# A fused pooling-attention and ResMLP kernel: the channel MLP cut into 512-token blocks across batch borders, q and k loaded as fp32 rows and cast on chip, the next batch's attention spread over both MLP products

## The chip, the cores and the metric

One core of a Trainium2 chip runs the whole kernel in one launch. The metric is device time in microseconds (us), the median of several executions. In the profile PE is TensorE's matmuls, PEld its weight loads, DVE VectorE, ACT ScalarE, POOL GpSimd, SP SyncE. A *period* below is the time from the first matmul of one MLP block's first product to that of the next block; I read these starts from the traces.

## The reference, cut to what matters

```python
# q, k, v: 8 batches x 8 heads x 576 tokens x 64, fp32
k_p = k.reshape(B, H, 72, 8, D).mean(axis=3)        # pooling by 8
v_p = v.reshape(B, H, 72, 8, D).mean(axis=3)
attn = softmax(scale * q @ k_p.T)
x = (attn @ v_p)  ->  (B, 576, 512)
tok = einsum('ts,bsd->btd', w_tok, alpha1 * x + beta1)   # token mix, 576 x 576
u = x + lam * tok
out = u + lam * (relu((alpha2 * u + beta2) @ w_ch1) @ w_ch2)   # channel MLP, 512 -> 2048 -> 512
```

## The kernel before

One batch of 576 tokens is one MLP block. TensorE's instruction stream weaves the MLP of batch b-1 with the attention of batch b; all engines take their instructions in a fixed order that a scheduler decides at build time. The parts that the argument touches (cuts marked):

```python
CR = [128, 128, 128, 128, 64]                  # token chunks of one batch

def load_qk_dma(b):                            # casting transfers: rows of 64 values
    for src, dst in ((q, q_bf), (k, k_bf)):
        for c in range(NCH):
            nc.gpsimd.dma_start(out=dst[0:rows, hf, c, :]..., in_=src[b, :, 128*c:128*c+rows, :]...)
...
nc.vector.memset(q_bf[64:65, :, 4, :], 0.0)    # a 65th row of zeros under the 64 remaining tokens
nc.vector.memset(k_bf[64:65, :, 4, :], 0.0)
...
def blk_F(b, hp):                              # the "q/k block", four per batch
    ...                                        # four transposes of q, 128 rows each
    nc.tensor.transpose(out=ps_qb[0:P, 0:65], in_=q_bf[0:65, hf, 4, h0:h0 + 128],
                        identity=identity_bf[0:65, 0:65])
    ...                                        # four pooling matmuls of k, 128 rows each
    nc.tensor.matmul(out=ps_kp[0:P, 64:72], lhsT=k_bf[0:65, hf, 4, h0:h0 + 128],
                     rhs=poolmat[0:65, 0:8])
...
def blk_V(b, hp):                              # the "v sums", two per head pair, on VectorE
    for hh in range(2):
        nc.vector.tensor_reduce(out=vp1[:, hh, 0:64], in_=v_hp[:, hh]..., op=ALU.add)
...
def blk_A(b, j):                               # first product: two halves of 288 columns
    for cc in range(4):
        for half in range(2):
            nc.tensor.matmul(out=ps_h[half][0:P, 0:288], lhsT=w1raw[:, cc, P*j:P*j+P],
                             rhs=u_fm[:, cc, n0:n0 + 288], ...)
    for half in range(2):
        nc.scalar.activation(out=Hj[:, n0:n0 + 288], in_=ps_h[half][0:P, 0:288], func=AF.Relu, ...)
...
def blk_B(b, tcx):                             # second product: five chunks, the last of 64 tokens
    for j in range(NJ):
        nc.tensor.matmul(out=ps_ch[0:tr, 0:DM], lhsT=s["Hj"][j][:, CO[tcx]:CO[tcx] + tr],
                         rhs=w2l[:, j, :], ...)
```

The softmax here doesn't subtract the row's maximum and nothing guards it: scores larger than these inputs give would overflow.

## Time and profile before

| | before |
|---|---|
| time, median | 438.4 us (438.4 to 439.0) |
| span of the profiled run, granted TensorE clock | 437.3 us, 0.973 |
| first MLP matmul | 62.0 us |
| period, batches 1 to 5 | 48.2 us |
| TensorE / VectorE / ScalarE busy | 89% / 52% / 46% |

TensorE is the bound, after a prologue in which it has little to do. The prediction shows the lines for that. Two more lines of the profile matter later. The first is the count of DMA packets:

```profile
DMA packets 88371, 35.37 MB, mean 81 GB/s; under 512 B 77776, under 2 KB 79824, under 8 KB 88336
```

The second is one q/k block in the timeline of TensorE in the kernel before. The columns are the start, the time until the group's last end, engine, line, operation, out<-in, the rows and columns of the array that the weights take, and the shape.

```profile
207.78 0.40 PE L209 MATMUL ps_qa<-identity_bf,q_bf 128*128 128x128 bf16 x4
208.02 0.20 PE L213 MATMUL ps_qb<-identity_bf,q_bf 65*128 65x65 bf16 x1
208.05 0.25 PE L220 MATMUL ps_kp<-poolmat,k_bf 128*128 128x16 bf16 x4
208.16 0.17 PE L222 MATMUL ps_kp<-poolmat,k_bf 65*128 65x8 bf16 x1
```

Matmuls overlap, so their durations must not be added; the starts tell what each costs. The 65-row transpose holds TensorE from 208.02 to 208.05 us, about 30 ns, and the whole block until the next MLP matmul, at 208.18 us, takes 0.40 us.

### The profile page before, as it was taken

How to read it: one execution, taken by the hardware profiler on the slowest of the kernel's cores; microseconds unless marked ns; L12 is line 12 of the kernel's file. 1: busy time of each engine (PE TensorE's matmuls, PEld its weight loads, DVE VectorE, ACT ScalarE, POOL GpSimd, SP SyncE). 2: the span in 40 equal slices, each digit the busy share in tenths (PEclk: the TensorE clock that was granted, in tenths of full speed). 3: DMA queues.
4: the chain of work that ended last, by engine and by line, in shares of the span. 5: the costliest groups of instructions: out<-in, count | busy, mean ns of one | idle time of the engine just before them, and what ended most of it. 6: DMA issues, size and time to landing. Idle time of an engine off the chain costs nothing.

```text
span 437.3 us, 7370 instructions
## 1 busy us (share of the span) xinstructions
PE 387.7 (89%) x2881; PEld 237.6 (54%) x2881; DVE 229.3 (52%) x598; ACT 202.6 (46%) x564; POOL 96.0 (22%) x128
## 2 busy tenths in 40 slices
PE   0166769999899989998999989998999989998996
PEld 0045257644675457644774457544764467545742
DVE  2378795776167643666077633874177514444011
ACT  1055139701892059602991079403980189205910
POOL 7574442810044000810063002700000000000000
PEclk9995779999999999999999999999999999999999
DMA  9999999972059200941089200921001100010011
GB/s 130 220 174 207 214 177 162 111 151 64 2 53 176 86 12 1 140 145 43 2 76 164 75 13 19 166 80 36 1 1 72 38 1 1 36 63 12 1 48 61
DMA packets 88371, 35.37 MB, mean 81 GB/s; under 512 B 77776, under 2 KB 79824, under 8 KB 88336
## 3 DMA queue, kind: packets, MB, share of 16 engines
q0 software_dynamic: 81280, 23.08, 48.7%
q1 hardware_dynamic: 5248, 9.44, 6.3%
q10 hardware_dynamic: 1808, 2.38, 2.0%
q8 instruction: 22, 0.36, 0.3%
q14 instruction: 13, 0.11, 0.1%
HBM read 39.08 MB, written 9.44 MB: 111 GB/s over the span
## 4 chain that ended last, share of the span: by engine, by line
PE 69%; DVE 12%; ACT 11%; DMA 4%; POOL 2%; issue 2%; POOLq 0%
PE ps_ch L346 29%; PE ps_h L331 23%; PE ps_tok L302 8%; ACT Hj L337 6%; DVE u_bf L308 3%; DVE out_sb L306 3%; PE ps_sc L247 3%; DMA k_bf<-in_k_dram 2%; DVE vp L233 2%; ACT ET L250 2%; PE ps_uT L317 2%; PE ps_av L263 2%; ACT qT L211 1%; DMA wt_sb<-in_moe_w_tok_dram 1%; DVE out_sb L350 1%
## 5 line engine op out<-in xcount | busy, mean ns | idle before, releaser
L331 PE MATMUL ps_h<-u_fm,w1raw 128*128 128x288 bf16 x1024 | 149.9, 288 | 1.1
L346 PE MATMUL ps_ch<-w2l,Hj 128*128 128x512 bf16 (+1 forms) x640 | 146.4, 379 | 0.0
L337 ACT ACTIVATE Hj<-ps_h,bias_cols 128x288 bf16<-128x288 f32 x256 | 113.0, 502 | 7.7 <-PE ps_h L331 5.2
L331 PEld LDWEIGHTS <-w1raw 128*128 128x128 bf16 x1024 | 96.8, 98 | 33.8 <-issue 6.0
L346 PEld LDWEIGHTS <-Hj 128*128 128x128 bf16 (+1 forms) x640 | 61.6, 100 | 66.1 <-issue 0.4
L320 ACT COPY u_fm<-ps_uT 128x512 bf16<-128x512 bf16 (+1 forms) x40 | 21.7, 542 | 157.8 <-PE ps_uT L317 157.8
L233 DVE TENSOR_REDUCE vp<-v_hp 72x64 f16<-72x512 f32 x64 | 63.9, 1007 | 7.0 <-DMA v_hp<-in_v_dram 7.0
L350 DVE TENSOR_TENSOR out_sb<-out_sb,ps_ch 128x512 f32<-128x512 f32 (+1 forms) x40 | 27.4, 685 | 73.2 <-PE ps_ch L346 73.1
L270 DVE RECIPROCAL rec<-ps_av 128x4 f32<-128x4 f32 x64 | 11.3, 177 | 92.6 <-PE ps_av L266 92.6
L79 POOL DMA_DIRECT2D v_hp<-in_v_dram x32 | 22.6, 708 | 164.8 <-DVE vp L233 159.3
L302 PE MATMUL ps_tok<-xs_tm,wtT 128*128 128x512 bf16 (+3 forms) x200 | 51.9, 393 | 4.6 <-DVE xs_tm L279 3.9
L250 ACT ACTIVATE ET<-ps_sc 72x288 f16<-72x288 f32 x128 | 44.7, 408 | 19.9 <-PE ps_sc L247 19.7
L306 DVE TENSOR_TENSOR out_sb<-x_tm,ps_tok 128x512 f32<-128x512 f32 (+1 forms) x40 | 27.3, 683 | 18.3 <-PE ps_tok L302 18.0
L63 POOL DMA_DIRECT2D k_bf<-in_k_dram x40 | 33.8, 890 | 8.8 <-DMA w2raw<-in_moe_w_ch_dram 3.5
L63 POOL DMA_DIRECT2D q_bf<-in_q_dram x40 | 34.1, 873 | 6.2 <-DMA v_hp<-in_v_dram 3.4
L302 PEld LDWEIGHTS <-wtT 128*128 128x128 bf16 (+3 forms) x200 | 18.4, 102 | 28.6 <-issue 9.1
L209 PE MATMUL ps_qa<-identity_bf,q_bf 128*128 128x128 bf16 x128 | 14.1, 236 | 16.4 <-POOL identity_bf L105 12.9
L317 PE MATMUL ps_uT<-identity_bf,u_bf 128*128 128x128 bf16 (+1 forms) x160 | 15.0, 216 | 15.1 <-DVE u_bf L308 15.1
L308 DVE TENSOR_TENSOR u_bf<-out_sb,al_bc 128x512 bf16<-128x512 f32 (+1 forms) x40 | 27.5, 688 | 1.2
L247 PE MATMUL ps_sc<-qT,kpT 128*72 128x288 bf16 x128 | 28.1, 305 | 0.0
L273 DVE TENSOR_TENSOR x_tm<-ps_av,rec 128x256 f32<-128x256 f32 x64 | 26.1, 408 | 0.0
L279 DVE TENSOR_TENSOR xs_tm<-x_tm,lamal_bc 128x256 bf16<-128x256 f32 x64 | 26.1, 407 | 0.0
(54 smaller groups left out, 244.5 us busy)
## 6 DMA issues: line engine op xcount, KB each, us to landing
v_hp<-in_v_dram POOLq DMA_DIRECT2D x32, 288.0 KB, 4.8
out_dram<-out_sb SPq DMA_DIRECT2D x32, 256.0 KB, 2.0
q_bf<-in_q_dram POOLq DMA_DIRECT2D x32, 128.0 KB, 4.4
k_bf<-in_k_dram POOLq DMA_DIRECT2D x32, 128.0 KB, 4.5
w1raw<-in_moe_w_ch_dram POOLq DMA_DIRECT2D x4, 512.0 KB, 11.0
w2raw<-in_moe_w_ch_dram POOLq DMA_DIRECT2D x4, 512.0 KB, 15.0
wt_sb<-in_moe_w_tok_dram ACTq DMA_DIRECT2D x4, 288.0 KB, 9.6
out_dram<-out_sb SPq DMA_DIRECT2D x8, 128.0 KB, 2.2
```

Source lines behind the costliest of these rows:

```text
L63: nc.gpsimd.dma_start(out=dst[0:rows, hf, c, :].rearrange("p (h d) -> p h d", d=D), in_=src[b, :, 128 * c:128 * c + rows, :].rearrange("h ...
L233: nc.vector.tensor_reduce(out=vp1[:, hh, 0:64], in_=v_hp[:, hh].rearrange("g p d -> g d p"), axis=mybir.AxisListType.X, op=ALU.add)
L247: nc.tensor.matmul(out=ps_sc[0:SPg, 0:288], lhsT=kpT[:, hh, :], rhs=qT[:, n0:n0 + 288])
L250: nc.scalar.activation(out=ET[:, n0:n0 + 288], in_=ps_sc[0:SPg, 0:288], func=AF.Exp, bias=0.0, scale=0.125)
L273: nc.vector.tensor_tensor(out=x_tm[:, 0:4, dd:dd + 64], in0=av[:, 0:4, 0:64], in1=rec[:, 0:4].unsqueeze(2).to_broadcast((P, 4, 64)), op=AL ...
L302: nc.tensor.matmul(out=ps_tok[0:tr, 0:DM], lhsT=wtT[0:kk, sc, CO[tcx]:CO[tcx] + tr], rhs=xs_tm[0:kk, sc, :], start=(sc == 0), stop=(sc == 4))
L306: nc.vector.tensor_tensor(out=s["out_sb"][0:tr, tcx, :], in0=st["x_tm"][0:tr, tcx, :], in1=ps_tok[0:tr, 0:DM], op=ALU.add)
L308: nc.vector.tensor_tensor(out=s["u_bf"][0:tr, tcx, :], in0=s["out_sb"][0:tr, tcx, :], in1=al2_bc[0:tr, :], op=ALU.mult)
L331: nc.tensor.matmul(out=ps_h[half][0:P, 0:288], lhsT=w1raw[:, cc, P * j:P * j + P], rhs=u_fm[:, cc, n0:n0 + 288], start=(cc == 0), stop=(cc ...
L337: nc.scalar.activation(out=Hj[:, n0:n0 + 288], in_=ps_h[half][0:P, 0:288], func=AF.Relu, bias=bias_cols[:, j:j + 1], scale=1.0)
L346: nc.tensor.matmul(out=ps_ch[0:tr, 0:DM], lhsT=s["Hj"][j][:, CO[tcx]:CO[tcx] + tr], rhs=w2l[:, j, :], start=(j == 0), stop=(j == NJ - 1))
L350: nc.vector.tensor_tensor(out=s["out_sb"][0:tr, tcx, :], in0=s["out_sb"][0:tr, tcx, :], in1=ps_ch[0:tr, 0:DM], op=ALU.add)
```

## The change

The intent: cut 4608 tokens into nine blocks of 512 instead of eight of 576 (the fifth chunk of 64 tokens wasted half of each matmul); evict 512 columns with one ScalarE instruction instead of two of 288; load q and k in wide fp32 rows on a hardware queue and cast on chip; and place the attention of the next batch beside both MLP products instead of mostly the first. The kernel was rewritten; this is the core of the diff, with cuts marked "...".

```diff
-        for src, dst in ((q, q_bf), (k, k_bf)):
-                nc.gpsimd.dma_start(
-                    out=dst[0:rows, hf, c, :].rearrange("p (h d) -> p h d", d=D),
...
+            nc.sync.dma_start(
+                out=raw[:, i, :, 0:4, :].rearrange("p h c d -> p h (c d)"),
+                in_=two[:, 0:512, :].rearrange("h (p c) d -> p h (c d)", c=4))
...
+            eng.tensor_copy(out=bf[:, i, 0:4].rearrange("p c h d -> p h c d"),
+                            in_=raw[:, i, :, 0:4, :])
+            eng.tensor_copy(out=bf[0:REM, i, 4], in_=raw[0:REM, i, :, 4, :])
...
-            nc.tensor.transpose(... in_=q_bf[0:65, hf, 4, h0:h0 + 128], identity=identity_bf[0:65, 0:65])
+        nc.tensor.transpose(out=ps_q[0:P, 512:576], in_=bf[0:REM, 0, 4],
+                            identity=identity_bf[0:REM, 0:REM])
...
+    for b in range(0, B, 2):
+        chunks += [(b, c) for c in range(4)]
+        chunks += [(b + 1, c) for c in range(4)]
+        chunks += [(b, 4)]
...
-                                 rhs=u_fm[:, cc, n0:n0 + 288],
+            nc.tensor.matmul(out=ps_h, lhsT=w1[:, cc, P * j:P * j + P], rhs=u_fm[n][:, cc, :],
+                             start=(cc == 0), stop=(cc == 3))
...
+        for hp in range(4):
+            todo.append((-1.0 + 3.5 * hp, lambda hp=hp: cast_qk(b, hp, (nc.gpsimd, nc.gpsimd))))
+            todo.append((1.5 + 3.5 * hp, lambda hp=hp: att_F(b, hp)))
+            todo.append((2.0 + 3.5 * hp, lambda hp=hp: att_V(b, hp)))
+        for h in range(H):
+            todo.append((14.5 + 1.0 * h, lambda h=h: att_S(b, h)))
+            todo.append((16.6 + 1.0 * h, lambda h=h: att_AV(b, h)))
```

REM is 64. A chunk (b, 4) holds the remainders of two batches. The numbers in the last lines are positions among the 32 steps of one MLP block (16 of the first product, 16 of the second); they set the program's order only, and the scheduler, which builds each engine's queue from it, may still move an instruction where its inputs allow it.

## The prediction

> **What bounds the kernel now.** I read the page's engine and slice rows first, then busy time by stage, then the chain of work that ended last, in order of time.
>
> ```profile
> PE 387.7 (89%) x2881; PEld 237.6 (54%) x2881; DVE 229.3 (52%) x598; ACT 202.6 (46%) x564; POOL 96.0 (22%) x128
> ...
> PE   0166769999899989998999989998999989998996
> PEclk9995779999999999999999999999999999999999
> DMA  9999999972059200941089200921001100010011
> ```
>
> TensorE is busy for nine tenths of nearly every slice from the seventh on, at the full clock; the DMA engines are full for the first 75 us and mostly idle afterwards. So there are three regimes, and the stage table (span, then PE, PEld, DVE, ACT, POOL busy, granted clock, DMA share, GB/s) separates them:
>
> ```profile
> 0.00:62.00 62.00, 27.93 (x240) 18.51 (x241) 39.44 (x99) 16.79 (x49) 34.78 (x51) 0.84 1.43 189
> ...
> 206.80:255.00 48.20, 46.56 (x349) 28.29 (x349) 26.49 (x71) 24.48 (x70) 11.20 (x14) 1.00 0.55 74
> ...
> 399.90:437.30 37.40, 33.23 (x210) 20.35 (x208) 3.43 (x5) 14.73 (x33) 0.00 (x0) 1.00 0.09 32
> ```
>
> A prologue of 62 us, until the first channel-MLP matmul; seven periods of 48.2 us, one batch's MLP woven with the next batch's attention; a tail of 37.4 us with MLP alone. The tail gives clean matmul prices:
>
> ```profile
> 399.93 15.81 PE ps_h L331 x128
> 415.74 17.40 PE ps_ch L346 x80
> ```
>
> 15.81 us / 128 = 123.5 ns for 288 columns and 217.5 ns for 512; inside a stage eight of the first kind take 0.98 us (122.5 ns) and sixteen of the second 3.46 us (216.3 ns). The same chain inside a period shows what PE waits for:
>
> ```profile
> 206.82 0.69 DVE u_bf L308
> 207.57 0.30 PE ps_uT L317 x4
> 207.89 0.37 ACT u_fm L320
> 208.26 0.54 ACT qT L211
> 209.27 0.33 ACT Hj L337
> 209.67 0.49 ACT Hj L337
> 210.16 0.47 ACT qT L211
> 211.09 1.67 ACT Hj L337 x4
> 212.76 0.58 ACT ET L250 x2
> ```
>
> At the batch border it is VectorE (the last chunk of u) and then, for the first 7 us of the first product, ScalarE's evictions, not TensorE. A price list for one period (timeline starts, next to next): first product 128 x 0.1225 = 15.7; second 80 x 0.2163 = 17.3; token mix 25 x 0.216 = 5.4; scores 8 x 0.24 = 1.9; attention times v 8 x 0.15 = 1.2; q transpose and k pooling 4 x 0.40 = 1.6; transposes of u 1.1. Sum 44.2, so **4.0 us of each 48.2 us period is TensorE waiting**, although "busy" shows only 1.6 us of idle, because busy durations overlap.
>
> **What the Trainium skill says.** "TensorE: Matmul & The Clock Gate", section Back-to-back issue gap, gives N/2.4 + 2.5 ns for a warm matmul: 122.5 and 215.8 ns for 288 and 512 columns, and the trace agrees (122.5, 216.3). The same section also says a stream sustains about 131 ns at N = 512; this trace does not, and I use 216.3. The price does not depend on the number of rows of the result, so the 64-token fifth chunk costs a full 128-row one: 16 x 216 ns = 3.46 us per batch (the chain has 3.57 for it). "VectorE: DVE Perf Modes", section The TRN2 errata, gives ScalarE 172 + N cycles at 1.2 GHz from PSUM: 383 ns for 288, 570 ns for 512. Four evictions of 288 take 1.67 us in the chain, about 0.39 apart: agreement. "DMA: Bandwidth & Descriptors", section Specifications, asks for at least 512 B for line rate. The trace agrees in kind: of 88,371 packets 77,776 are under 512 B, nearly all of them q and k rows of 64 bf16 values, and their queue is busy 48.7% of the engines' time. "GPSIMD Engine Reference", section Engine selection, calls one-input elementwise work on GpSimd roughly line rate; no run here shows a cast there yet.
>
> **The change part by part.**
>
> *MLP in nine blocks of 512 tokens.* The 4608 tokens become 9 x 512 instead of 8 x 576, two 64-token remainders sharing a chunk. First product: 9 x 64 x 0.2163 = 124.6 us instead of 8 x 15.7 = 125.4. Second: 9 x 64 x 0.2163 = 124.6 instead of 8 x 17.3 = 138.4. **Saved on TensorE: 14.7 us**, on the path.
>
> *One 512-wide eviction instead of two of 288.* In the old first product ScalarE has 32 x 0.39 = 12.5 us of ReLU, about 4 x 1.0 us of q, k copies and 14 x 0.29 us of exp: 20.6 us, in a phase that lasts 21.1 us. It is as full as TensorE there. New: 16 x 0.57 = 9.1 plus 4 x 0.65 of qT = 11.7 us, against 13.8 + 1.6 us of TensorE. The exps move beside the second product, kpT copies go to VectorE. ScalarE stops binding.
>
> *Spread attention.* VectorE's work in a period is about 28 us, as before (v sums 8 us, x 4.5, xs 3, u and output 10). The instruction order of the built kernel has 19 second-product matmuls (4.1 us) between the last attention times v and the token mix; VectorE's chain for x and xs in that gap is about 3 us (two v sums included), so it should be hidden. After the first two mixes 7 more matmuls (1.5 us) hide the conversion of u. Exposed I expect the last transposes of u, 0.5 to 1 us. TensorE's sum per period: 13.84 + 13.84 + 5.4 + 1.9 + 1.2 + 1.6 + 1.0 = 38.8. I add 1.4 us of waits by judgement, a third of what the old one has: **40.2 us**.
>
> *q, k as fp32 rows, cast on chip.* Packets of 256 B read and 128 B written become 1 KB. By packet durations (32 ns for the old kind; 86 to 98 ns for 1 to 2 KB) a batch's q and k fall from 19 to about 9 us of all engines. In the steady part that was hidden and is worth nothing; casts on GpSimd, some 10 us in 40 (my estimate), are hidden too. It counts in the prologue alone.
>
> *Prologue.* Data first: batch 0 is 3.5 MB, w_tok 1.3, then w1, w2 (8.4 MB at the source) and batch 1's 3.5 MB compete; the old kernel moves about 190 GB/s as landed there. The last piece needed, batch 1's first v, which VectorE's order places before the last u, should land near 45 to 50 us. VectorE: 13 v sums x 0.93 = 12.1, u 8 x 0.65 = 5.2, x 4.2, xs 2.9, w_tok's sums and copies 6.5, casts 2.4, kpT and qT 2.8, one w2 scaling 2.2, constants 2.2: 40.5 us, starting near 9 us where the old one gets its first broadcast rows (9.90). With 4 us of waits, last transpose and copy: **53.5 us** to the first MLP matmul, against 62.2.
>
> *Sum.* 53.5 + 7 x 40.2 = 281.4, plus 2.4 in block 0 (a mix of 1.1, bias columns 1.3), two blocks with MLP alone 2 x 27.7 = 55.4, a tail of 4.2 after the last matmul as before (437.3 - 433.1), and 1.1 from span to time (438.4 - 437.3): **398.0 us**. Of the 40.4 us gained, 14.7 are matmuls saved, about 18 waits (7 x 2.6), 8.7 the prologue, less 2.
>
> **Rivals.**
>
> *VectorE becomes the bound of the second product.* It gets x, xs, u, output and v sums in about 25 us, some 20 us of it busy; a late xs stalls the mix. For it: v sums stand between urgent work in its order, and the old chain already has v sum, x, xs ahead of the mix (240.99 to 242.78). Against: 19 matmuls of cover. It would make the period 42 to 43 and the time 412.
>
> *The prologue stays bound by transfers.* The same bytes from HBM, w1 and w2 early, [...]and DMA engines that were full. Then the first MLP matmul comes at 60 to 62 and the time is 406. Against: q and k packets were the slow ones.
>
> *Nothing stalls.* 38.9 us a period and a prologue of 49: 384 us.
>
> *The transfer change pays in every period.* Against: from 158 us on the DMA engines are half idle and no long wait on q, k or v is listed. I give it nothing.
>
> **Range and chances.** Prologue 53.5 +6/-5, periods 281.4 +13/-8; taken as independent, with the matmul savings certain, 387 to 411 holds 8 in 10. For less than 2% gain the time would have to exceed 429.7, which needs both rivals and more: 0.03. Slower: 0.01.
>
> **What would show it right or wrong.** First-product matmuls at 216 ns, x576, one ReLU of 512 columns below 0.6 us start to start; a period of 40 us with ScalarE gone from the chain in the first product; the first MLP matmul near 53.5 us with VectorE in the chain before it. Wrong if the chain of a period shows xs or v sums ahead of the mix for over 2 us, GpSimd casts ahead of q's transposes, or transfers of v or w_tok in the prologue after 50 us.

## The result, and the profile after

The changed kernel took **439.1 us** (437.6 to 439.9, 4 runs), the kernel before 438.7 us (438.4 to 439.3) on the same chip: a ratio of 1.000, 95% interval 0.998 to 1.003. (Ratios in this document are the mean time of one kernel's fast runs over that of the other's in the same rounds, so not quite the ratio of the medians.) The expected gain of 40 us did not come, though less work was done, as the page of the changed kernel shows (its busy row of TensorE, the row of the granted clock in 40 slices, the packets):

```profile
PE 370.4 (85%) x2315; PEld 191.5 (44%) x2358; DVE 233.2 (53%) x484; ACT 181.8 (42%) x348; POOL 71.9 (17%) x139
...
PEclk9999859999999999999999999999999999999999
...
DMA packets 43436, 44.71 MB, mean 103 GB/s; under 512 B 12624, under 2 KB 33104, under 8 KB 43408
```

TensorE is busy 17 us less, ScalarE 21 us less, and the packets are halved; the time went into waiting. The stage table (as in the prediction: start and end, length, busy time of PE, PEld, DVE, ACT and POOL, granted clock, DMA share, GB/s) says where: prologue, blocks 4 and 6, and the first block with MLP alone.

```profile
0.00:64.46 64.46, 25.68 (x178) 17.05 (x180) 42.84 (x113) 12.87 (x29) 23.68 (x44) 0.89 1.03 228
245.27:290.68 45.41, 41.03 (x265) 21.19 (x269) 26.89 (x54) 20.63 (x40) 6.56 (x16) 1.00 0.25 77
333.78:375.49 41.71, 40.70 (x266) 21.22 (x270) 20.39 (x46) 20.63 (x40) 0.00 (x0) 1.00 0.08 26
375.49:403.11 27.62, 27.52 (x129) 12.51 (x129) 2.48 (x4) 11.58 (x17) 0.00 (x0) 1.00 0.10 39
```

The block with MLP alone takes 27.62 us (27.7 predicted). The prologue is 11 us longer than predicted. And of two blocks with the same work, block 4 takes 3.7 us more than block 6; the differences visible here are VectorE, 26.89 against 20.39 us busy, and GpSimd, 6.56 us against none (its casts for a later batch). Three things can be read from the trace before any experiment.

**The q/k block costs twice what it did.** TensorE's timeline in the changed kernel, to be held against the one of before:

```profile
215.79 0.39 PE L233 MATMUL ps_q<-identity_bf,qk_bf 128*128 128x128 bf16 x4
216.11 0.20 PE L235 MATMUL ps_q<-identity_bf,qk_bf 64*128 64x64 bf16 x1
216.24 0.29 PE L245 MATMUL ps_kp<-pool_main,qk_bf 128*128 128x64 bf16 x4
216.46 0.18 PE L247 MATMUL ps_kp<-pool_rem,qk_bf 64*128 64x8 bf16 x1
216.57 0.61 PE L351 MATMUL ps_h<-u_fm,w 128*128 128x512 bf16 x2
```

From start to start the remainder's transpose now holds TensorE 0.13 us (0.03 before) and the whole block 0.78 us (0.40 before), although it is the same number of matmuls. Two differences are visible: "64*128" where "65*128" stood, since the kernel before carried a 65th row of zeros, and 64 columns instead of 16 in the pooling of k (e1 below keeps the 64 columns and so tests the rows alone). The Trainium skill, "TensorEngine Tiling (Array Packing)", section Key Properties, says that a change of tiling mode drains TensorE; its section Available Configurations lists 64 x 128 under row tiling, apart from 128 x 128. My reading is that 65 rows fall into the 128-row mode and 64 don't; four switches a block at about 0.1 us are the 0.38 us (each of the four starts after a switch comes 0.08 to 0.11 us later than in the kernel before, counted from the start before it).

**VectorE has the v sums in the wrong place.** Waits of TensorE and VectorE in block 4 of the changed kernel (total us, how often, the longest; 245 to 291 us), and then the chain of work at the end of block 3 (start, us, what):

```profile
DVE kpT L249 <- PE ps_kp L247: 12.1, 4, 3.8
...
PE ps_uT L340 <- DVE u_bf L329: 2.2, 2, 1.3
PE ps_tok L324 <- DVE xs L297: 1.8, 1, 1.8
```

```profile
233.41 0.92 DVE vp L256
234.32 0.60 DVE xs L297
...
235.12 0.60 DVE u_sb L369
235.72 1.87 DVE vp L256 x2
237.60 1.19 DVE u_sb L327 x2
238.79 0.61 DVE u_bf L329
239.45 0.40 PE ps_uT L340 x4
```

VectorE stands idle 12.1 us in the first product, waiting for the next pooled k, while TensorE waits 4.0 us for xs and u in the second, where sums ("vp") of the *next* batch stand ahead of them in VectorE's queue. VectorE doesn't wait for v there, so v had landed; the scheduler put the sums where it found room (my reading of its order). All eight sums of a period lie in the second product in blocks 0 to 5. Block 6 has none, since there is no further batch; its 3.7 us are the first measure of what they cost.

**In the prologue VectorE waits for v of the next batch.** The chain of the changed kernel up to the last transposes before the MLP:

```profile
39.31 11.87 DMA qk_raw<-in_q_dram
...
51.19 5.72 DMA v_hp<-in_v_dram
...
56.94 1.93 DVE vp L256 x2
58.87 0.59 DVE u_sb L327
59.46 0.92 DVE vp L256
...
63.18 0.62 PE ps_uT L340 x4
```

VectorE has the last two pieces of batch 0's u still to make, but two sums of batch 1 stand before the first and one before the second, and their v lands at 56.9 us; VectorE waits 7.2 us. The transfer itself took 5.7 us: SyncE's queue, which issues q, k and v, came to it only at 51.2 us, behind the issues of batch 1's q and k. Issuing v earlier would be another cure; no run tries it. TensorE waits with VectorE, and its granted clock falls to 0.68 over the last 19 us of the prologue (45.0 to 64.46), and is still 0.70 over the first 4.5 us of block 0.

### The profile page after: what moved, and what is told of

Same layout as the page of the kernel before. It is cut to its first block, busy times and chain, and to the rows that moved or that the text cites. A ratio compares the mean times of both kernels' runs of the same rounds, so it can differ in the third digit from the quotient of the medians.

```text
span 435.9 us, 6112 instructions
## 1 busy us (share of the span) xinstructions
PE 370.4 (85%) x2315; PEld 191.5 (44%) x2358; DVE 233.2 (53%) x484; ACT 181.8 (42%) x348; POOL 71.9 (17%) x139
## 4 chain that ended last, share of the span: by engine, by line
PE 55%; DVE 29%; DMA 12%; issue 2%; SPq 1%; ACT 0%
PE ps_h L351 29%; PE ps_ch L364 11%; DVE vp L256 10%; PE ps_tok L324 6%; DMA qk_raw<-in_q_dram 6%; DVE x_tm L290 5%; DVE xs L297 4%; DVE u_sb L369 4%; DMA v_hp<-in_v_dram 3%; PE ps_uT L340 2%; DMA b2col<-in_moe_beta_dram 2%; DVE u_sb L327 2%; DVE u_bf L329 2%; DVE rec L288 1%; PE ps_q L233 1%
## 5 line engine op out<-in xcount | busy, mean ns | idle before, releaser
L364 PE MATMUL ps_ch<-w,Hj 128*128 128x512 bf16 x553 | 136.5, 379 | 1.7 <-issue 0.6
L351 PE MATMUL ps_h<-u_fm,w 128*128 128x512 bf16 x557 | 132.1, 381 | 1.8 <-ACT u_fm L342 0.7
L354 ACT ACTIVATE Hj<-ps_h,bias_cols 128x512 bf16<-128x512 f32 x144 | 98.9, 687 | 57.0 <-PE ps_h L351 54.0
L351 PEld LDWEIGHTS <-w 128*128 128x128 bf16 x576 | 53.7, 98 | 59.9 <-issue 1.8
L89 POOL CAST qk_bf<-qk_raw 128x512 bf16<-128x512 f32 x60 | 42.5, 709 | 224.3 <-issue 153.4
L364 PEld LDWEIGHTS <-Hj 128*128 128x128 bf16 x576 | 51.8, 98 | 52.0 <-issue 1.6
L324 PE MATMUL ps_tok<-xs,wtT 128*128 128x512 bf16 (+2 forms) x199 | 50.6, 391 | 10.4 <-DVE xs L297 10.2
L267 PE MATMUL ps_sc<-qT,kpT 128*72 128x288 bf16 x128 | 27.6, 307 | 9.7 <-DVE kpT L249 9.7
L327 DVE TENSOR_TENSOR u_sb<-x_tm,ps_tok 128x512 f32<-128x512 f32 (+1 forms) x40 | 26.8, 681 | 14.4 <-PE ps_tok L324 14.4
L290 DVE TENSOR_TENSOR x_tm<-ps_av,rec 128x320 f32<-128x320 f32 x64 | 29.9, 480 | 0.3
L329 DVE TENSOR_TENSOR u_bf<-u_sb,al_bc 128x512 bf16<-128x512 f32 (+1 forms) x40 | 27.7, 705 | 0.8
```

Of the source, the lines that this page charges most:

```text
L89: eng.tensor_copy(out=bf[:, i, 0:4].rearrange("p c h d -> p h c d"), in_=raw[:, i, :, 0:4, :])
L267: nc.tensor.matmul(out=ps_sc[0:SPG, 0:288], lhsT=kpT_pool[hp][:, hh, :], rhs=st["qT"][hp][:, n0:n0 + 288])
L290: nc.vector.tensor_tensor(out=x[:, :, dd:dd + D], in0=av[:, :, 0:64], in1=rec.unsqueeze(2).to_broadcast((P, 5, D)), op=ALU.mult)
L324: nc.tensor.matmul(out=ps_tok[p0:p1, 0:DM], lhsT=wtT[0:kk, at, P * c:P * c + (p1 - p0)], rhs=xs[0:kk, sc, :], start=(sc == 0), stop=(sc == 4))
L327: nc.vector.tensor_tensor(out=s["u"][p0:p1, :], in0=st1[b]["x"][p0:p1, c, :], in1=ps_tok[p0:p1, 0:DM], op=ALU.add)
L329: nc.vector.tensor_tensor(out=s["u_bf"][p0:p1, :], in0=s["u"][p0:p1, :], in1=al2_bc[p0:p1, :], op=ALU.mult)
```

## The experiments

Every kernel gave a correct result. Times of before in the same rounds were 439.1 to 439.7 us. "First" is the time of the first MLP matmul, then block 0, then the periods of the odd and of the even ones among blocks 1 to 5 (an even block transposes one chunk of u more). These are read from the one profiled run of each kernel; the time is a median.

| run | first | block 0 | odd | even | time |
|---|---|---|---|---|---|
| changed kernel | 64.5 | 49.2 | 43.1 | 45.4 | 439.1 |
| e1_rows65 | 68.6 | 48.5 | 41.55 | 43.8 | 431.0 |
| e2_vfirst | 57.7 | 50.7 | 43.1 | 45.4 | 432.6 |
| e3_vlater | 65.6 | 46.8 | 40.5 | 41.7 | 421.2 |
| e4_both | 68.6 | 44.6 | 38.95 | 40.15 | 411.9 |
| e5_w2late | 58.7 | 46.9 | 38.95 | 40.15 | 405.8 |
| e6_b2late | 59.7 | 46.9 | 38.95 | 40.15 | 406.0 |
| e7_castdma | 75.5 | 50.8 | 43.1 | 45.4 | 450.2 |
| e8_attnA | 60.0 | 48.6 | 39.85 | 40.7 | 410.8 |
| e9_w2dma | 57.2 | 45.3 | 38.95 | 40.15 | 401.9 |
| e10_v2x_early | 65.0 | 51.9 | 44.9 | 47.1 | 450.3 |
| e11_v2x_late | 60.2 | 45.3 | 40.3 | 41.5 | 412.3 |
| e12_w2dma_b2 | 57.1 | 46.9 | 38.95 | 40.15 | 402.3 |
| e13_order | 65.4 | 46.3 | 40.7 | 42.35 | 422.8 |

**e1: the 65th row back.** Theory: the switch between 64 and 128 rows is the cost. Rival: the time saved is lost again in a wait for VectorE. The edit also makes the cast buffers constant, so that their row of zeros stays.

```diff
+    for t in bf_pool:
+        nc.vector.memset(t[64:65, :, 4], 0.0)
-        nc.tensor.transpose(out=ps_q[0:P, 512:576], in_=bf[0:REM, 0, 4],
+        nc.tensor.transpose(out=ps_q[0:P, 512:577], in_=bf[0:REM + 1, 0, 4],
-        nc.tensor.matmul(out=ps_kp[0:P, 64:72], lhsT=bf[0:REM, 1, 4],
+        nc.tensor.matmul(out=ps_kp[0:P, 64:72], lhsT=bf[0:REM + 1, 1, 4],
```

> The changed kernel, with the 64-row remainder of q and k padded to 65 rows (row 64 zero, six constant cast buffers in place of six rotating ones), as the kernel before had it. Theory A (drain): each q/k block of the changed kernel has four switches between matmuls with 128 and with 64 contraction rows, and each holds TensorE about 0.1 us; a block takes 0.78 us where the old one took 0.40. Padded, it takes 0.40 to 0.45 again; a period shrinks by 1.4 us, the time by 9 to 12 us, to 427 to 430 us. Rival B (hidden): the time TensorE saves in the first product is lost again before the token mix, where it waits for VectorE: the period stays at 43 to 45.5 us and the time within 3 us of 439.

Each period fell by 1.55 us, and the time by 8.1 us, 1 us less than the range that I had written; the ratio to before is 0.981 (0.979 to 0.984). The timeline of this run shows the remainder back at 0.04 us:

```profile
164.45 0.20 PE L240 MATMUL ps_q<-identity_bf,qk_bf 65*128 65x65 bf16 x1
164.49 0.28 PE L250 MATMUL ps_kp<-pool_main,qk_bf 128*128 128x64 bf16 x4
164.60 0.17 PE L252 MATMUL ps_kp<-pool_rem,qk_bf 65*128 65x8 bf16 x1
```

The theory holds; a matmul with *more* rows is cheaper here. The first MLP matmul came 4.2 us later than in the changed kernel, which more than accounts for the miss: the scheduler moved other instructions (its trace has the same wait as e4's, below, 8.9 us).

**e2 and e3: the v sums behind the k copies of their own batch.** e2 does it for batch 1 alone (the prologue), e3 for batches 2 to 7 alone (the periods), e4 for all, with the 65th row. The edit orders the queue, nothing else:

```diff
+    def att_V_late(b, hp):
+        if b == 1:                     # e3: b >= 2;  e4: b >= 1
+            with tc.issue_after(st1[b]["kp_ins"][hp]):
+                att_V(b, hp)
+        else:
+            att_V(b, hp)
```

> The changed kernel, with only batch 1's v sums queued on VectorE behind batch 1's k copies, so after batch 0's u. Theory A (queue order): VectorE stands for 7.2 us at 49.8 us for v of batch 1 and then mixes 6 us of its sums among batch 0's last u; without them the first MLP matmul comes at 52 to 55 us instead of 64.5 and the time falls by 8 to 12 us, to 427 to 431. Rival B (transfers): q, k and v of batch 1 and the weights arrive too late anyway, TensorE waits for them in the first block instead, and the time falls by less than 4 us.

> The changed kernel, with the v sums of batches 2 to 7 queued on VectorE behind the k copies of their own batch (in the first product of the block), not in the second product of the block before. The scheduler then also puts the token mixes between second-product matmuls in another order. Theory A (VectorE bound in the second product): waits for xs before the mix (1.6 to 2.0 us a period) and for u before its transposes (0.8 to 2.5 us) mostly vanish, as in block 6, which has no later v sums and loses 3.0 us where the others lose 4.6 and 6.7. Periods of 43.1 and 45.4 us become 40.5 to 41.5; the time falls by 12 to 18 us, to 421 to 427. Rival B (latency of the batch border): the waits are the chain mix, u, transpose, copy itself, whatever VectorE does beside it; they stay, and the time falls by less than 5 us.

> All three together: 65 rows, and the v sums of batches 1 to 7 behind their own k copies. If the three causes are separate and add, the time falls by 30 to 38 us, to 401 to 409, with the first MLP matmul at 52 to 55 us and periods of 39 to 40 us. If one hides another it stays above 412.

e2: the first MLP matmul came at 57.7 us, 6.7 us earlier but not at the expected 52 to 55, and the time, 432.6 us, missed its range by 1.6 us. Into the place of the sums the scheduler drew two more scalings of w2 (2.3 us each) than the changed kernel has there, and block 0 grew by 1.5 us; the ratio is 0.985 (0.981 to 0.990). e3: periods of 40.5 and 41.7 us as expected, 0.959 (0.957 to 0.960). Its block 4 takes as long as block 6, 41.72 us, with VectorE busy 27.77 us and GpSimd 6.60, so it is not the amount of work of either that made block 4 long. e4: the two cures add up to 0.1 us in the periods (six of them: 261.8 us in the changed kernel, 252.5 in e1, 246.7 in e3, 237.3 here), but the first MLP matmul was at 68.6 us, so the time missed the range that I had written. Its timeline of VectorE has the reason:

```profile
38.53 2.29 DVE L216 TENSOR_TENSOR w<-w,lam_bc 128x2048 bf16<-128x2048 bf16 x1 [8.81 <-DMA w<-in_moe_w_ch_dram]
```

One scaling of w2, not needed for another 50 us, stood in VectorE's queue ahead of batch 0's x and waited 8.8 us for its transfer. The same error with another instruction.

**e5 and e6: the scalings of w2, and the small copy of beta2, moved behind.** e5 is e4 with the scalings behind batch 1's k copies; e6 also moves the copy whose transfer kept VectorE 3.7 us in the changed kernel.

```diff
-                todo.append((8.2 + 2 * g, lambda g=g: scale_w2(g)))
+                todo.append((8.2 + 2 * g, lambda g=g: scale_w2_late(g)))   # issue_after(kp_ins of batch 1)
-        nc.vector.tensor_copy(out=b2c_bf, in_=b2col)                        # e6 only
+    with tc.issue_after(att_x_ins[0]):                                      # e6 only
+        nc.vector.tensor_copy(out=b2c_bf, in_=b2col)
```

> The kernel with both cures (65-row remainders, v sums behind the k copies), and with the four scalings of w2 queued on VectorE behind batch 1's k copies. Theory A (in that kernel one scaling of w2 stood in VectorE's in-order queue ahead of batch 0's last work and waited 8.8 us there for its transfer, which put the first MLP matmul at 68.6 us): the first MLP matmul comes at 55 to 58 us, periods stay at 38.95 and 40.15 us, the time is 398 to 403 us. Rival B (that wait only hid a transfer that the prologue needs anyway): the first MLP matmul stays after 64 us and the time is 407 us or more. Rival C (the scalings come too late where they now stand and the second product of block 0 waits for them): first MLP matmul 55 to 58, block 0 lasts over 50 us instead of 44.6.

> As the run before (both cures, late w2 scalings), and the small copy of beta2, whose transfer landed at 14.8 us while VectorE stood 3.7 us before it, is queued behind batch 0's last xs. Theory A (VectorE is the chain of the prologue from its first instruction on): the first MLP matmul comes 2.5 to 3.7 us earlier than in the run before and the time falls as much. Rival B (what follows waits for transfers of batch 0 anyway): 0 to 1 us.

e5: 405.8 us, 0.924 (0.920 to 0.927), the first MLP matmul 9.9 us earlier than in e4. It misses both its ranges, by 0.7 us in the prologue and by 2.8 us in time, since block 0 also grew by 2.4 us: 1.6 us of that is TensorE waiting for a k copy that stands behind two late scalings. e6 gained nothing (its rival was right), since VectorE then waits for w_tok, as e5's timeline shows:

```profile
35.64 0.69 DVE L181 TENSOR_REDUCE wsum<-wt_sb 128x1 f32<-128x512 f32 x1 [2.48 <-DMA wt_sb<-in_moe_w_tok_dram]
...
40.10 0.22 DVE L182 TENSOR_REDUCE wsum<-wt_sb 128x1 f32<-128x64 f32 x1 [3.77 <-DMA wt_sb<-in_moe_w_tok_dram]
```

**e9 and e12: w2's transfers issued later.** In e5 the transfers of w2 start at 24 to 30 us, beside that of w_tok. e9 issues them behind GpSimd's casts for batch 1; e12 adds e6's edit.

```diff
-    for g in range(4):
-        load_w2(g)
+                todo.append((-0.9 + 0.01 * g, lambda g=g: load_w2_late(g)))   # issue_after(cast of batch 1)
```

> Both cures, late w2 scalings, and the four transfers of w2 issued behind GpSimd's first cast of batch 1 (some 43 us) instead of at 24 to 30 us. Theory A (what is left of the prologue waits for w_tok, which landed at 40.1 us because w2's 4.2 MB of reads share the DMA engines with it): w_tok lands 5 to 10 us earlier, the first MLP matmul comes at 50 to 55 us instead of 58.7, time 398 to 402 us. Rival B (VectorE's own work fills the prologue by then): 57 to 59 us and 404 to 407 us. Rival C (w2 then comes too late for block 0): block 0 over 50 us instead of 46.9.

> The run before in this set plus the small copy of beta2 moved out of VectorE's way (it gained nothing where w_tok's transfer was the bound). If VectorE is the bound of the prologue once w2 is out of the way: 1.5 to 3.7 us earlier than the run before. If transfers still bound it: within 1 us.

The last wait for w_tok ended at 36.6 us instead of 40.1, less than expected, and the first MLP matmul came only 1.5 us earlier, at 57.2 us, where the rival (VectorE's own work fills the prologue) had put it; the time is in the theory's range. A transpose of w_tok on TensorE still waits until 39.8 us. The profile names a transfer of k as what ended that wait, which the transpose does not read. It reads the sums of w_tok's rows, and VectorE's write of these ended at 39.76 us, after its work on x had stood before it from 37.45 us on; that is the likelier release. After that, transposes, token mixes and u follow one another on TensorE and VectorE. Block 0 is 1.65 us shorter (not so in e12). At 401.9 us, ratio 0.915 (0.913 to 0.917), **e9 is the fastest of all, 8.5% below the kernel before**. e12 is the same within its spread (402.3), so moving the small copy pays neither in e5 nor in e9, although the profile's chain runs through its transfer.

**e7: the transfer part undone.** q and k in 64-value rows through GpSimd's casting queue, without casts on chip; all else as in the changed kernel.

```diff
-            nc.sync.dma_start(out=raw[:, i, :, 0:4, :]..., in_=two[:, 0:512, :]...)
+                nc.gpsimd.dma_start(out=bf[:, i, 0:4, h, :],
+                                    in_=one[0:512, :].rearrange("(p c) d -> p c d", c=4))
```

> The changed kernel with its transfer part undone: q and k come in 128-byte pieces through the casting queue of GpSimd as in the kernel before, without the casts on chip; all else as changed. If the wide fp32 transfers are worth what the prediction gave them: steady periods unchanged (43.1 and 45.4 us, within 0.5), and the first MLP matmul 3 to 10 us later than the 64.5 us of the changed kernel, so 442 to 450 us. Rival (the casts on GpSimd and their waits cost as much as the pieces): prologue within 2 us of 64.5. Rival (the pieces also delay the steady part): periods longer by over 1 us.

The steady periods are the same to 0.02 us; the first MLP matmul is 11.0 us later (just outside the expected range) and block 0 is 1.6 us longer; 450.2 us, ratio 1.024 (1.020 to 1.027). So the wide transfers are worth 11 us in the prologue and nothing afterwards, in this kernel's order. Taken with the result, the other parts lengthened the prologue by 13.5 us (75.5 against 62.0 before).

**e8: the attention beside the first product alone** (e5 otherwise).

```diff
-            todo.append((14.5 + 1.0 * h, lambda h=h: att_S(b, h)))
-            todo.append((16.6 + 1.0 * h, lambda h=h: att_AV(b, h)))
+            todo.append((3.0 + 1.75 * h, lambda h=h: att_S(b, h)))
+            todo.append((5.6 + 1.75 * h, lambda h=h: att_AV(b, h)))
```

> Both cures and the late w2 scalings, with the scores, the exponentials and attention times v put beside the first MLP product alone instead of beside both; x in the first product too. If spreading the attention is worth something by ScalarE's load (in the first product 16 x 0.57 + 4 x 0.65 of qT + 8 x 0.5 of exponentials = about 16 us in a stretch that lasts some 18 us of TensorE): periods 1 to 2.5 us longer than 38.95 and 40.15 us, 408 to 418 us. Rival (512-wide evictions alone freed ScalarE, the spread adds nothing): periods within 0.5 us, time within 4 us of the first run of this set. Rival (x comes early, so the waits for xs and u before the batch border vanish): periods shorter by 0.5 to 1.5 us.

Periods grew by 0.9 and 0.5 us, less than I expected; only with 3 us more in prologue and block 0 is the time, 410.8 us, in the range. Spreading pays 3.6 us in the six periods, not more, and not by ScalarE's load: among the 65 longest of the 75 pieces of the chain over block 3 (190 to 231 us) none is ScalarE's; the longest stretch off TensorE, 199.8 to 205.8 us, is VectorE's, v sums and x among them. So with 512-wide evictions ScalarE is off the path even with the exps beside the first product.

**e10 and e11: twice the sums.** If the place counts and not the amount, the same extra work on VectorE must cost something where the scheduler puts it and little behind the k copies. e10 doubles the sums of batches 2 to 7 in the changed kernel, e11 in e5.

```diff
-            for hh in range(2):
+            for hh in (0, 1, 0, 1) if b >= 2 else (0, 1):
```

> The changed kernel with each v sum of batches 2 to 7 computed twice (the same result), where the scheduler places them: some 7.4 us more VectorE work in a period, standing among x, xs and u of the batch before. Theory A (the place of the sums sets the period, since VectorE is late there): the periods of blocks 1 to 5 grow from 43.1 and 45.4 us by 4 to 8 us. Rival B (the sums only fill idle time, the waits for xs and u have another cause): by less than 1 us.

> The kernel with both cures and late w2 scalings, each v sum of batches 2 to 7 computed twice, behind the k copies; TensorE's order of instructions is the same as without. Theory A (the place, not the amount, sets the period): periods stay within 1.5 us of 38.95 and 40.15 us although VectorE has as many us more to do as in the run before. Rival B (VectorE's load bounds the period wherever it stands): they grow by 4 to 8 us.

Both have two runs each and one profile. e11: +1.35 us on periods, within its range. e10: +1.8 and +1.7 us, between my two ranges: I had assumed that all the new sums would stand in the second product. In the trace only four or five more do (12 in odd blocks, 13 in even ones, against 8); the others went to the free start of the first. Counting sums in the second product orders the blocks of three traces:

| sums in the second product | 0 | 8 | 13 |
|---|---|---|---|
| even block | 41.7 us (block 6; e3 too) | 45.4 | 47.1 |
| odd block (12 instead of 13) | 40.5 (e3) | 43.1 | 44.9 |

That is 0.3 to 0.5 us for each sum of about 1 us that stands there, and eight in the first product are free: e3 has them all there. With 14 in the first product and two in the second (e11) the extra ones cost 1.35 us.

**e13: TensorE's order held.** When the sums move, the scheduler also reorders TensorE: in the changed kernel two token mixes stand together after 19 second-product matmuls and the last transposes come together; in e3 each mix is separated by four matmuls. Block 6 of the changed kernel has e3's order too, so neither comparison separates VectorE's lateness from TensorE's order. e13 is e3 with TensorE's instructions in blocks 1 to 5 chained into exactly the changed kernel's order.

```diff
+        steps = [lambda: ch(0, 1, 2), lambda: mix_T(b, 0), lambda: mix_T(b, 1),
+                 lambda: ch(3, 4, 5, 6, 7, 8, 9), lambda: mix_uT(key[0]), lambda: mix_T(b, 2), ...]
+        for do in steps:
+            with tc.issue_after(last_pe()):
+                do()
```

> The changed kernel with the v sums of batches 2 to 7 behind the k copies, as in the run that moved them alone (periods 40.5 and 41.7 us there), but with TensorE's instructions in blocks 1 to 5 held in exactly the order that the changed kernel has (periods 43.1 and 45.4 us). Theory A (what costs is that VectorE delivers xs and u late): the periods stay within 0.7 us of 40.5 and 41.7 us, the time is 420 to 425 us. Rival B (what costs is TensorE's order, which bunches mixes and transposes): the periods go back to within 0.7 us of 43.1 and 45.4 us, and the time is 434 to 440 us. In between: both, in proportion.

40.7 and 42.35 us, 422.8 us, ratio 0.962 (0.960 to 0.965). Of the 15.1 us that e3 gains in blocks 1 to 5, 13.4 us (88%) remain with the changed kernel's order on TensorE. So VectorE's lateness is the main cause; the order that the scheduler made of it adds the rest (1.75 us), most of it in even blocks, where transposes bunch at the end.

## Why the prediction was wrong

Its sum, term by term, against the changed kernel and against the two corrected ones (us):

| term | predicted | changed | e5 | e9 |
|---|---|---|---|---|
| prologue | 53.5 | 64.5 | 58.7 | 57.2 |
| block 0 | 42.6 | 49.2 | 46.9 | 45.3 |
| blocks 1 to 6 | 241.2 | 261.8 | 237.3 | 237.3 |
| two blocks of MLP alone | 55.4 | 55.0 | 55.0 | 55.0 |
| after the last matmul's start | 4.2 | 5.4 | 5.4 | 5.4 |
| span to time | 1.1 | 3.2 | 2.4 | 1.8 |
| sum | 398.0 | 439.1 | 405.8 | 401.9 |

(The prediction counts its tail from the end of the last matmul; so counted, the two bare blocks take 55.4 us and the tail 5.0. Span to time is 3.2 us in the changed kernel because the profiled run was 1.5 us faster than the median.)

That e9 ends near the 398.0 us is partly luck: its periods are 3.9 us shorter than predicted, its prologue and block 0 6.4 us longer. Slips in the prediction's working that move nothing: it sets 62.2 us for the old first MLP matmul where its own table has 62.0, its parts add up to a gain of 39.6 us and not 40.4, and the DMA engines are full for eight slices, 87 us, not 75.

*MLP in nine blocks: right.* The two bare blocks took 27.6 and 27.4 us for 27.7 predicted. The 14.7 us of matmuls were saved, and were lost elsewhere.

*One eviction of 512, ScalarE no longer the bound: right.* A ReLU of 512 columns takes 0.58 us start to start where another instruction follows at once (block 4, 251.45 to 252.03), below the 0.6 set as a sign; in block 4 no wait of TensorE on a ReLU is listed, and e8 shows ScalarE could even take the exps back at a price of 0.5 to 0.9 us.

*"Q transpose and k pooling 1.6", and with it TensorE's sum of 38.8: wrong.* I carried the price of 0.40 us for a q/k block over from the kernel before, whose remainder has 65 rows. With 64 it is 0.78 us, 3.1 us a period. The prediction doesn't mention that the diff drops the zero row. e1: 1.55 us a period, 9.4 us in six.

*"So it should be hidden", said of VectorE's chain before the mix: wrong, and the largest error.* I compared a chain of 3 us, two v sums included, with 19 matmuls of cover (4.1 us). In block 3 VectorE finished xs 5.9 us after the last attention times v began (229.24 to 235.12), since earlier x, another xs and an output were still in its queue; TensorE stood 1.4 us before the mix and 0.6 us before the transposes. All eight sums stand in the second product, and delay x, xs and u one after the other; a local chain can be covered while the engine as a whole is behind. e3 puts it at 15.1 us in blocks 1 to 5, and e13 shows that 13.4 of them are VectorE. The *rival* that I named, "VectorE becomes the bound of the second product", with periods of 42 to 43 us, is what happened; without the drains of e1 the periods would be 41.5 and 43.8. Its cause was in the same words: sums between urgent work. I set only the cover of 19 matmuls against it, and a mean load (28 us in 40) that looked safe.

*Prologue, "with 4 us of waits": wrong.* VectorE's sum of work, 40.5 us, fits (42.8 us busy measured); but one wait for v is 7.2 us. I had even named this v as "the last piece needed", at 45 to 50 us; it landed at 56.9. e2 puts the wait at 6.7 us of the prologue. 53.5 is not reached by e9 either: there w_tok's last transfer is waited for until 36.6 us, and then VectorE's own work until 39.8; how much of the remaining 3.7 us each costs I did not test.

*Transfers worth nothing in the steady part: right* (e7). Their value in the prologue, 11 us, is there, hidden under the other parts.

*Block 0* is 6.6 us longer than predicted. About half is what each period has (3.4 us on average); at a clock of 0.70, 4.5 us lose another 1.4 (an estimate: 30% of them). The remaining 1.8 us I did not trace.

*The chances.* I wrote that a gain of under 2% "needs both rivals and more: 0.03". The first rival came, the second in its effect (64.5 us, for another reason than the rate of transfers), and the q/k drain on top. They were not independent: two of the three are the same thing, an instruction without urgency queued in front of an urgent one on VectorE.

## What to carry to other kernels

When an engine's mean load is safe, read its order instead: a non-urgent instruction can be queued ahead of urgent work, and if its input is late the whole queue stands; pin it behind something that you know to be late enough, and look again, since the next filler takes its place. When a change drops padding, price the unpadded shape from a trace that has it, not from the padded one.

## What the Trainium skill lacked or had wrong

- "TensorEngine Tiling (Array Packing)" names the drain at a change of mode but gives no price, and doesn't say that a lone 64-row matmul in a stream of 128-row ones pays it twice: about 0.1 us each way here (0.78 against 0.40 us for a block of ten matmuls, two of them with 64 rows), and that 65 rows avoid it. I did not open this page before predicting.
- "TensorE: Matmul & The Clock Gate" gives, in section Back-to-back issue gap, about 131 ns for a sustained matmul of 512 columns; two bare MLP blocks of 128 such matmuls took 27.6 and 27.4 us, 216 ns each, which is what the same section gives for an isolated one.
- "GPSIMD Engine Reference" calls one-input work on GpSimd roughly line rate; here casts of 128 x 512 fp32 to bf16 took 0.61 us there in the median (0.71 in the mean, the slowest 4.0), against 0.41 us on VectorE.
- No page puts a figure on what a build-time order does to an engine that takes its queue in order: here VectorE stood 7.2 us (v), 8.8 us (w2) and 3.7 us (beta2) for one transfer each; moving the first two paid 6.7 and 9.9 us up to the first MLP matmul, moving the third nothing.
